# Two ways to transpose q in a Linformer attention and FFN kernel: where each batch's transpose runs, and when it is sent off

## The chip, the cores and the metric

The kernel runs on one core of a Trainium2 chip. The metric is the device time of one execution in microseconds (us), as the median of several runs. A profile of one execution stands beside it; its span is the time from the first to the last instruction.

Names used below: PE or TensorE does matmuls and transposes and writes to PSUM; PEld is its weight load; DVE is VectorE; ACT is ScalarE; POOL is GpSimd, which here issues all loads; SP is SyncE, which here issues the stores and the DMA transposes.

## The reference

Eight batches, eight heads, sequence 1024, head size 64. Keys and values are projected along the sequence from 1024 to 64 rows, then comes plain softmax attention, and its output (8192 tokens x 512) goes through a two-layer FFN with the quick GELU.

```python
k_proj = np.einsum('ks,bhsd->bhkd', E, k)            # 64 x 64 per head
v_proj = np.einsum('ks,bhsd->bhkd', F, v)
scores = np.matmul(q, k_proj.transpose(0, 1, 3, 2)) / np.sqrt(64)
attn   = softmax(scores)                             # over 64 columns
x      = np.matmul(attn, v_proj)                     # heads side by side: 8192 x 512
h      = x @ w_in                                    # 512 x 2048
out    = (h * sigmoid(1.702 * h)) @ w_out            # 2048 x 512
```

## The kernel before

The work is cut into 16 token blocks ("layers" below) of 512 tokens, two to a batch. Layer j runs the first FFN product (`ffn1`, 16 slots of four matmuls of 512 columns, L286) and then the second (`ffn2`, 8 slots of eight matmuls, L297). The attention of later layers is done in the gaps: a list `fill` hangs small pieces behind the slots, `at(j, slot, piece)`. Slots 0 to 15 are those of `ffn1`, O = 16 and up those of `ffn2`. Layer 0 has its `ffn1` cut in two halves, so that its `ffn2` begins at slot Q = 32.

The scores need q with the head dimension on the partitions. For that q has to be transposed. Batch 0 does it on TensorE (`q_tr`), batches 1 to 7 by DMA (`q_dma`):

```python
    def load_q(b):
        qt[b] = ldpool.tile([P, J, H, D], BF16, name="q_sb")
        qv = q[b].rearrange("h (p j) d -> p j h d", p=P)
        for j in range(J):
            nc.gpsimd.dma_start(out=qt[b][:, j], in_=qv[:, j])

    def load(b):
        load_kv(k, kt, b, "k_sb")
        load_q(b)
        load_kv(v, vt, b, "v_sb")
# ...
    def q_tr(g):
        def go():
            if g == 0:
                qT[0] = att.tile([P, J, HP, P], BF16, name="qT")
            t_ps = f_tile([P, 2, HP, P], BF16)
            for jj in range(2):
                for h in range(H):
                    r = h % 2 * D
                    nc.tensor.transpose(t_ps[r:r + D, jj, h // 2, :], qt[0][:, h, 2 * g + jj, :], ident)
            cp = nc.scalar.copy if g == 1 else nc.vector.tensor_copy
            cp(qT[0][:, 2 * g:2 * g + 2], t_ps)
        return go

    def q_dma(b):
        def go():
            qT[b] = att.tile([P, J, HP, P], BF16, name="qT")
            nc.sync.dma_start_transpose(out=qT[b].rearrange("r j p s -> r (j p) s"),
                                        in_=qt[b].rearrange("s j h d -> s (j h d)"))
        return go

    def four(outs, lhsTs, rhss):

        for i, ro in ((0, (LO, HI)), (1, (HI, LO))):
            for ri, r in zip((LO, HI), ro):
                nc.tensor.matmul(outs[i][r], lhsTs[i][ri], rhss[i][ri], start=True, stop=True)

    def scores(h, u):
        b, c = divmod(h, NB2)

        def go():
            if u == 0:
                expT[h] = att.tile([P, HP, TB], BF16, name="expT", bufs=3)
            s_ps = [f_tile([P, TB]) for _ in range(2)]
            four(s_ps, [kts[b % 2][:, 2 * u + i, :] for i in range(2)],
                 [qT[b][:, c * JB:(c + 1) * JB, 2 * u + i, :] for i in range(2)])
            for i in range(2):
                nc.scalar.activation(expT[h][:, 2 * u + i, :], s_ps[i], AF.Exp, scale=scale)
        return go
```

`load(b)` fills the buffers two batches ahead. The pool of `q_sb` has two buffers, so a load waits for the transpose that reads the buffer's former content; `qT` has two buffers as well. The PSUM pool of `f_tile` has four banks, which `ffn1`, `ffn2`, the scores and the transposes share.

The projection of k and v of a batch, and what follows it:

```python
    def proj(b):
        def go():
            kvps[b] = f_tile([P, H, D])
            for j in range(J):
                for e, r in enumerate((LO, HI)):
                    nc.tensor.matmul(kvps[b][r], eft[:, j, e * KP:(e + 1) * KP],
                                     (kt, vt)[e][b][:, :, j, :],
                                     start=(j == 0), stop=(j == J - 1))
        return go
# ...
    def kv_out(b):
        def go():
            ps = kvps.pop(b)
            k_b = att.tile([KP, H, D], BF16, name="k_b")
            nc.vector.tensor_copy(k_b, ps[LO])
            if b > 1:
                nc.sync.dma_start_transpose(out=kts[b % 2], in_=k_b.rearrange("k h d -> k (h d)"))
            v_part(b, ps, slice(0, 2))
            kbs[b] = k_b
        return go
```

From batch 2 on, `k_b` is transposed by a small DMA transpose on the same SyncE queue (`kts`); batch 1 does it on TensorE (`k_tr`).

The places of these pieces:

```python
    at(0, 0, tok(0, 2))
    at(0, 1, tok(0, 3))
    at(0, 4, x_tr(0, 2))
    at(0, 6, x_tr(0, 3))
    at(0, 18, q_tr(2))
    at(0, 20, q_tr(3))
    at(0, Q, scores(1, 0), scores(1, 1), gelu_table)
    for t in range(JB):
        at(0, Q + 2 + t, tok(1, t))
        at(0, Q + 3 + t, x_tr(1, t))
    at(1, 3, q_dma(1))
    at(1, 8, proj(1))
    at(1, 9, kv_out(1))
    at(1, 10, lambda: k_tr(1, kbs[1], 0), q_dma(2))
    for u in range(2):
        at(1, O + u, scores(2, u))
        at(1, O + 3 + u, scores(3, u))
        at(2, O + u, scores(4, u))
        at(2, O + 3 + u, scores(5, u))
    for t in range(JB):
        at(1, O + 2 + t, tok(2, t))
        at(1, O + 3 + t, x_tr(2, t))
    at(2, 1, norm(3, 0))
    at(2, 11, norm(3, 1))
    for b in range(2, B):
        j = max(2, NB2 * b - 3)
        at(j, 2, proj(b))
        at(j, 3, kv_out(b))
        if b > 2:
            at(j, 4, q_dma(b))
    for j in (1, 2):
        at(j, O + 5, gelu_table)
    at(2, O + 5, norm(4, 0))
    at(3, 4, norm(4, 1))
    for j in range(3, NBLK - 2):
        for u in range(2):
            if j + 3 < NBLK:
                at(j, O + 5 * u, scores(j + 3, u))
            at(j, O + 5 * u, norm(j + 2, u))
        if j + 3 < NBLK:
            at(j, O + 6, gelu_table)

# ...
    for j in range(NBLK):
        if j % NB2 == 0 and j // NB2 + 2 < B:
            load(j // NB2 + 2)
        halves = 2 if j == 0 else 1
        for i in range(halves * FC):
            hf, fc = divmod(i, FC)
            ffn1(j, fc, slice(hf * TB // halves, (hf + 1) * TB // halves))
            filled(j, i)
        for s in range(2 * JB):
            ffn2(j, s // 2, s % 2)
            filled(j, halves * FC + s)
```

Of the kernel before, what the change touches and what calls it, by code (L numbers as in the profile page):

```python
# [10 lines left out]
BF16 = mybir.dt.bfloat16  # L11
# [6 lines left out]
def kernel(ctx, tc, q, k, v, E, F,  # L18
                                                     moe_w_in, moe_w_out, out):
    nc = tc.nc  # L20
    B, H, S, D = q.shape
    KP, _ = E.shape
    DM, DFF = moe_w_in.shape
    P = 128
    J = S // P
    NB2 = S // 512
    HP = H // 2
# [10 lines left out]
    att = ctx.enter_context(tc.tile_pool(name="att", bufs=2))  # L38
# [11 lines left out]
    kt, vt, qt = {}, {}, {}  # L50
# [29 lines left out]
    ident = consts.tile([P, P], BF16)  # L80
# [32 lines left out]
    def f_tile(shape, dt=F32):  # L113
        return ps_f.tile(shape, dt, name="f_ps")

    def warm(n):
        w_ps = f_tile([P, TB])
        for _ in range(n):
            nc.tensor.matmul(w_ps, zeros[:, :P], zeros, start=True, stop=True)  # L119
# [6 lines left out]
    t_ps = f_tile([P, J, 2 * KP], BF16)  # L126
# [6 lines left out]
    kvps, kbs, qT, expT, xT = {}, {}, {}, {}, {}  # L133
# [10 lines that stand above are left out]
# [32 lines left out]
# [8 lines that stand above are left out]
            kbs[b] = k_b  # L184
        return go

    def q_tr(g):
        def go():
            if g == 0:
                qT[0] = att.tile([P, J, HP, P], BF16, name="qT")  # L190
            t_ps = f_tile([P, 2, HP, P], BF16)
            for jj in range(2):
                for h in range(H):
                    r = h % 2 * D
                    nc.tensor.transpose(t_ps[r:r + D, jj, h // 2, :], qt[0][:, h, 2 * g + jj, :], ident)
            cp = nc.scalar.copy if g == 1 else nc.vector.tensor_copy
            cp(qT[0][:, 2 * g:2 * g + 2], t_ps)
        return go

    def q_dma(b):  # L200
# [24 lines that stand above are left out]
# [42 lines left out]
    def x_tr(h, t):  # L267
        def go():
            x_sb = xs.pop((h, t)).rearrange("s h d -> s (h d)")
            n_ps = ps_n.tile([P, KC, P], BF16, name="n_ps")  # L270
            for c in range(KC):
                nc.tensor.transpose(n_ps[:, c, :], x_sb[:, c * P:(c + 1) * P], ident)  # L272
            cp = nc.scalar.copy if (h, t) == (0, 0) else nc.vector.tensor_copy
            cp(x_of(h)[:, :, t * P:(t + 1) * P], n_ps)
        return go
# [33 lines left out]
    def at(j, slot, *fs):  # L309
        fill.setdefault((j, slot), []).extend(fs)  # L310

    O = FC
    Q = 2 * FC
# [1 line left out]
        k_half(proj0(0, g), g)  # L315
        warm(3)
    for g in (0, 1):
        q_tr(g)()
    warm(4)
    for u in range(2):  # L320
        scores(0, u)()
# [9 lines left out]
    at(0, 1, tok(0, 3))  # L331
    at(0, 4, x_tr(0, 2))
    at(0, 6, x_tr(0, 3))
    at(0, 18, q_tr(2))
    at(0, 20, q_tr(3))
    at(0, Q, scores(1, 0), scores(1, 1), gelu_table)
    for t in range(JB):
        at(0, Q + 2 + t, tok(1, t))
        at(0, Q + 3 + t, x_tr(1, t))
    at(1, 3, q_dma(1))  # L340
    at(1, 8, proj(1))
    at(1, 9, kv_out(1))
    at(1, 10, lambda: k_tr(1, kbs[1], 0), q_dma(2))
# [10 lines left out]
    for b in range(2, B):  # L354
        j = max(2, NB2 * b - 3)
        at(j, 2, proj(b))
        at(j, 3, kv_out(b))
        if b > 2:
            at(j, 4, q_dma(b))
    for j in (1, 2):  # L360
        at(j, O + 5, gelu_table)
    at(2, O + 5, norm(4, 0))
# [55 lines left out]
```

The softmax here doesn't subtract the row's maximum and nothing guards it: scores larger than these inputs give would overflow.

## Time and profile before

| | |
|---|---|
| time, median of 3 runs | 528.34 us (527.36 to 529.83) |
| profiled span | 527.6 us, 6576 instructions |
| granted TensorE clock, mean | 0.996 |
| eight batches of FFN on TensorE: L297, L286 | 231.8 and 227.2 us busy |
| score, denominator and value matmuls (L211) | 13.6, 10.3 and 10.1 us busy |
| transposes of q: 7 by DMA, time to landing | median 12.4 us |

The page cuts the span into 40 slices of 13.2 us. Each digit is the busy share in tenths:

```profile
PE   6799989999999999999989999999999999999997
PEclk9999998999999999999999999999999999999999
DMA  9999999999999029950299205010150201010102
```

TensorE is near full except at the two ends. The granted clock dips in one slice, the seventh. The DMA engines are full for the first 13 slices (170 us), in which weights and the first batches are loaded, and then busy in bursts.

An idle time that a row shows in brackets is the time in which its engine did nothing just before, with what ended that idle time. Matmuls are pipelined, so the start-to-start distance of rows tells more than the length of one.

### The profile page before, as it was taken

The numbers are of one execution on the slowest core, as the hardware profiler recorded it, in microseconds if no ns is written. First come the engines' busy times: TensorE is split into PE (matmuls) and PEld (weight loads), VectorE is DVE, ScalarE is ACT, GpSimd is POOL, SyncE is SP. The second block draws the span as 40 slices with busy tenths as digits, with TensorE's granted clock in tenths as the row PEclk, the third lists the DMA queues.
The fourth block names the chain that finished last, engine by engine and source line by source line (L and its number), as shares of the span: only waits on it lengthen the run. The fifth ranks groups of instructions, "written<-read, shape, count | busy, mean of one in ns | idle before, by whom it ended". The sixth has DMA issues, their size and how long they took to land.

```text
span 527.6 us, 6576 instructions
## 1 busy us (share of the span) xinstructions
PE 508.6 (96%) x2798; PEld 230.8 (44%) x2798; DVE 243.9 (46%) x206; ACT 264.7 (50%) x433; POOL 75.9 (14%) x94
## 2 busy tenths in 40 slices
PE   6799989999999999999989999999999999999997
PEld 3475434444444444344434444444444444444443
DVE  2411212683966381746718275572818466470000
ACT  1466454465546546364563745556464646334351
POOL 6344314331050000500014000000000000000000
PEclk9999998999999999999999999999999999999999
DMA  9999999999999029950299205010150201010102
GB/s 168 200 203 182 244 141 195 179 208 163 167 132 185 0 81 158 109 136 1 91 155 152 88 2 148 18 80 1 78 88 0 81 0 81 1 80 2 80 0 81
DMA packets 116878, 54.83 MB, mean 104 GB/s; under 512 B 89712, under 2 KB 114288, under 8 KB 114928
## 3 DMA queue, kind: packets, MB, share of 16 engines
q0 software_dynamic: 83328, 29.37, 49.8%
q1 hardware_dynamic: 33440, 24.78, 17.7%
q8 instruction: 22, 0.36, 0.3%
q10 hardware_dynamic: 80, 0.26, 0.2%
q14 instruction: 8, 0.07, 0.0%
HBM read 59.24 MB, written 16.78 MB: 144 GB/s over the span
## 4 chain that ended last, share of the span: by engine, by line
PE 81%; DMA 16%; DVE 1%; POOL 1%; issue 1%; ACT 0%; SPq 0%; ACTq 0%; POOLq 0%
PE f_ps L297 41%; PE f_ps L286 32%; DMA qT<-q_sb 11%; DMA w_in_sb<-in_moe_w_in_dram 5%; PE f_ps L140 2%; PE f_ps L211 2%; PE d_ps L211 1%; PE n_ps L211 1%; DVE vq L173 0%; DVE k_b L180 0%; PE n_ps L272 0%; PE d_ps L257 0%; POOL v_sb L57 0%; POOL k_sb L57 0%; ACT o_sb L300 0%
## 5 line engine op out<-in xcount | busy, mean ns | idle before, releaser
L243 DVE RECIPROCAL rden<-d_ps 128x512 f32<-128x512 f32 x52 | 174.4, 3353 | 153.8 <-PE d_ps L211 153.8
L297 PE MATMUL f_ps<-w_out_sb,gT 128*128 128x512 bf16 x1024 | 231.8, 381 | 0.1
L286 PE MATMUL f_ps<-xT,w_in_sb 128*128 128x512 bf16 (+1 forms) x1088 | 227.2, 367 | 1.2 <-DMA w_in_sb<-in_moe_w_in_dram 0.6
L288 ACT ACTIVATE gT<-f_ps 128x512 bf16<-128x512 f32 (+1 forms) x272 | 155.7, 572 | 87.3 <-PE f_ps L286 86.1
L286 PEld LDWEIGHTS <-w_in_sb 128*128 128x128 bf16 x1088 | 104.8, 98 | 118.5 <-issue 4.9
L297 PEld LDWEIGHTS <-gT 128*128 128x128 bf16 x1024 | 97.8, 98 | 123.4 <-issue 12.9
L300 ACT COPY o_sb<-f_ps 128x512 f32<-128x512 f32 x64 | 37.6, 587 | 140.3 <-PE f_ps L297 130.5
L63 POOL DMA_DIRECT2D q_sb<-in_q_dram x56 | 49.1, 894 | 88.3 <-DMA qT<-q_sb 47.6
L223 ACT ACTIVATE expT<-f_ps 128x512 bf16<-128x512 f32 x64 | 34.7, 600 | 10.9 <-PE f_ps L211 10.8
L244 DVE TENSOR_TENSOR xT<-n_ps,rden 128x512 bf16<-128x512 f32 x52 | 36.0, 692 | 5.5
L57 POOL DMA_DIRECT2D k_sb<-in_k_dram x9 | 7.8, 866 | 102.1 <-PE f_ps L140 98.7
L211 PE MATMUL f_ps<-qT,kt 64*64 64x512 bf16 x128 | 13.6, 404 | 7.5 <-DMA qT<-q_sb 6.9
L223 ACT ACT_TABLE_LOAD x13 | 16.7, 1283 | 5.9 <-PE f_ps L211 5.7
L227 ACT ACT_TABLE_LOAD x14 | 18.0, 1283 | 0.3
L262 DVE RECIPROCAL rd<-d_ps 128x4 f32<-128x4 f32 x24 | 4.2, 175 | 27.2 <-PE d_ps L257 27.2
L140 PE MATMUL f_ps<-k_sb,eft 128*64 128x512 bf16 x56 | 13.4, 382 | 0.0
L140 PE MATMUL f_ps<-v_sb,eft 128*64 128x512 bf16 x56 | 13.4, 382 | 0.0
L211 PEld LDWEIGHTS <-kt 64*64 64x64 bf16 x128 | 3.9, 103 | 21.1 <-issue 17.7
L263 DVE TENSOR_TENSOR x_sb<-d_ps,rd 128x256 bf16<-128x256 f32 x24 | 10.2, 425 | 0.8
L119 PE MATMUL f_ps<-zeros 128*128 128x512 bf16 x30 | 9.4, 450 | 1.2 <-DVE zeros L101 1.2
L211 PE MATMUL d_ps<-expT,ones 64*64 64x512 bf16 x104 | 10.3, 381 | 0.0
L211 PE MATMUL n_ps<-expT,vq 64*64 64x512 bf16 x104 | 10.1, 376 | 0.0
(45 smaller groups left out, 92.3 us busy)
## 6 DMA issues: line engine op xcount, KB each, us to landing
out_dram<-o_sb SPq DMA_DIRECT2D x15, 1024.0 KB, 3.9
k_sb<-in_k_dram POOLq DMA_DIRECT2D x7, 1024.0 KB, 16.8
q_sb<-in_q_dram POOLq DMA_DIRECT2D x56, 128.0 KB, 12.7
v_sb<-in_v_dram POOLq DMA_DIRECT2D x7, 1024.0 KB, 10.8
w_in_sb<-in_moe_w_in_dram POOLq DMA_DIRECT2D x8, 256.0 KB, 14.4
w_out_sb<-in_moe_w_out_dram POOLq DMA_DIRECT2D x4, 512.0 KB, 14.4
k_sb<-in_k_dram POOLq DMA_DIRECT2D x2, 512.0 KB, 7.5
q_sb<-in_q_dram POOLq DMA_DIRECT2D x2, 512.0 KB, 13.7
```

What stands on the lines that cost most here:

```text
L63: nc.gpsimd.dma_start(out=qt[b][:, j], in_=qv[:, j])
L140: nc.tensor.matmul(kvps[b][r], eft[:, j, e * KP:(e + 1) * KP], (kt, vt)[e][b][:, :, j, :], start=(j == 0), stop=(j == J - 1))
L211: nc.tensor.matmul(outs[i][r], lhsTs[i][ri], rhss[i][ri], start=True, stop=True)
L223: nc.scalar.activation(expT[h][:, 2 * u + i, :], s_ps[i], AF.Exp, scale=scale)
L227: nc.scalar.preload_act_table(AF.Gelu_apprx_sigmoid)
L243: nc.vector.reciprocal(rden, d_ps[i])
L244: nc.vector.tensor_tensor(x_of(h)[:, 2 * u + i, :], n_ps[i], rden, op=ALU.mult)
L263: nc.vector.tensor_tensor(xs[h, t][:, 4 * g:4 * g + 4, :], d_ps[:, :, :D], rd.to_broadcast([P, 4, D]), op=ALU.mult)
L286: nc.tensor.matmul(h_ps, w_in_sb[:, kc, fc * P:(fc + 1) * P], xT[j][:, kc, ts], start=(kc == 0), stop=(kc == KC - 1))
L288: nc.scalar.activation(gts[j][:, fc, ts], h_ps, AF.Gelu_apprx_sigmoid)
L297: nc.tensor.matmul(o_ps[0], gts[j][:, fc, n * P:(n + 1) * P], w_out_sb[:, fc, :], start=(fc == 0), stop=(fc == FC - 1))
L300: nc.scalar.copy(osb[j][:, n, :], o_ps[0])
```

## The change

Three things are done. Batch 1's q is transposed on TensorE, in four groups of eight transposes behind slots 2, 4, 6 and 8 of layer 1, with a copy to SBUF by VectorE for each; its DMA transpose goes. The DMA transposes of batches 3 to 7 are sent off at slot O of layer 2b - 4, the second half of the layer in front of the one that projects that batch's k (batch 2's stays at layer 1, slot 10). And the two halves of the scores of token block 1 stand behind two slots in place of one. The aim is that q's transpose is there when the scores want it.

```diff
--- before.py
+++ after.py
@@ -184,17 +184,24 @@
             kbs[b] = k_b
         return go
 
-    def q_tr(g):
+    def q_tr(b, g):
         def go():
             if g == 0:
-                qT[0] = att.tile([P, J, HP, P], BF16, name="qT")
+                qT[b] = att.tile([P, J, HP, P], BF16, name="qT")
             t_ps = f_tile([P, 2, HP, P], BF16)
             for jj in range(2):
-                for h in range(H):
-                    r = h % 2 * D
-                    nc.tensor.transpose(t_ps[r:r + D, jj, h // 2, :], qt[0][:, h, 2 * g + jj, :], ident)
-            cp = nc.scalar.copy if g == 1 else nc.vector.tensor_copy
-            cp(qT[0][:, 2 * g:2 * g + 2], t_ps)
+                j = 2 * g + jj
+                if b == 0:
+                    for h in range(H):
+                        r = h % 2 * D
+                        nc.tensor.transpose(t_ps[r:r + D, jj, h // 2, :], qt[0][:, h, j, :], ident)
+                else:
+                    for p in range(HP):
+                        nc.tensor.transpose(
+                            t_ps[:, jj, p, :],
+                            qt[b][:, j, 2 * p:2 * p + 2, :].rearrange("s t d -> s (t d)"), ident)
+            cp = nc.scalar.copy if b == 0 and g == 1 else nc.vector.tensor_copy
+            cp(qT[b][:, 2 * g:2 * g + 2], t_ps)
         return go
 
     def q_dma(b):
@@ -315,7 +322,7 @@
         k_half(proj0(0, g), g)
         warm(3)
     for g in (0, 1):
-        q_tr(g)()
+        q_tr(0, g)()
     warm(4)
     for u in range(2):
         scores(0, u)()
@@ -331,13 +338,15 @@
     at(0, 1, tok(0, 3))
     at(0, 4, x_tr(0, 2))
     at(0, 6, x_tr(0, 3))
-    at(0, 18, q_tr(2))
-    at(0, 20, q_tr(3))
-    at(0, Q, scores(1, 0), scores(1, 1), gelu_table)
+    at(0, 18, q_tr(0, 2))
+    at(0, 20, q_tr(0, 3))
+    at(0, Q, scores(1, 0))
+    at(0, Q + 1, scores(1, 1), gelu_table)
     for t in range(JB):
         at(0, Q + 2 + t, tok(1, t))
         at(0, Q + 3 + t, x_tr(1, t))
-    at(1, 3, q_dma(1))
+    for g in range(4):
+        at(1, 2 + 2 * g, q_tr(1, g))
     at(1, 8, proj(1))
     at(1, 9, kv_out(1))
     at(1, 10, lambda: k_tr(1, kbs[1], 0), q_dma(2))
@@ -356,7 +365,7 @@
         at(j, 2, proj(b))
         at(j, 3, kv_out(b))
         if b > 2:
-            at(j, 4, q_dma(b))
+            at(NB2 * b - 4, O, q_dma(b))
     for j in (1, 2):
         at(j, O + 5, gelu_table)
     at(2, O + 5, norm(4, 0))
```

## The prediction

> **What bounds the kernel now.** I read the busy shares and the chain of waits on the page first, then the list of who waited for whom, then the timeline of TensorE around each wait that this list names.
>
> ```profile
> PE 508.6 (96%) x2798; PEld 230.8 (44%) x2798; DVE 243.9 (46%) x206; ACT 264.7 (50%) x433; POOL 75.9 (14%) x94
> PE 81%; DMA 16%; DVE 1%; POOL 1%; issue 1%; ACT 0%; SPq 0%; ACTq 0%; POOLq 0%
> PE f_ps L297 41%; PE f_ps L286 32%; DMA qT<-q_sb 11%; DMA w_in_sb<-in_moe_w_in_dram 5%; PE f_ps L140 2%; PE f_ps L211 2%; PE d_ps L211 1%; PE n_ps L211 1%; DVE vq L173 0%; DVE k_b L180 0%; PE n_ps L272 0%; PE d_ps L257 0%; POOL v_sb L57 0%; POOL k_sb L57 0%; ACT o_sb L300 0%
> ```
>
> TensorE is the bound: busy 96%, every other engine at half or less. The chain puts 11% (56 us, as its answer in order of time has 10.6%) on the DMA transposes of q. The reader must not take that as what can be won: the chain follows the transposes back to their issue, and TensorE worked during most of that time. What it lost is in the list of waits (waiter, what was waited for: us in total, times, longest us):
>
> ```profile
> PE f_ps L211 <- DMA qT<-q_sb: 6.9, 4, 2.8
> POOL q_sb L63 <- DMA qT<-q_sb: 47.6, 4, 14.1
> PE f_ps L211 <- ACT expT L223: 0.5, 1, 0.5
> ```
>
> So the score matmuls (L211) stood still for q's transpose four times, 6.9 us in all. The 47.6 us of GpSimd are loads held back because their buffer was still being transposed; they cost nothing unless a matmul waits for what they load. The timeline of TensorE around the first and the fourth wait (start, us, engine, what, in brackets the idle time before):
>
> ```profile
> 75.07 1.89 PE L297 MATMUL f_ps<-w_out_sb,gT 128*128 128x512 bf16 x8
> 79.80 0.64 PE L211 MATMUL f_ps<-qT,kt 64*64 64x512 bf16 x4 [2.84 <-DMA qT<-q_sb]
> 80.37 3.31 PE L297 MATMUL f_ps<-w_out_sb,gT 128*128 128x512 bf16 x8
> 83.61 0.41 PE L211 MATMUL f_ps<-qT,kt 64*64 64x512 bf16 x4
> ```
>
> ```profile
> 271.05 1.89 PE L297 MATMUL f_ps<-w_out_sb,gT 128*128 128x512 bf16 x8
> 274.69 0.41 PE L211 MATMUL f_ps<-qT,kt 64*64 64x512 bf16 x4 [1.75 <-DMA qT<-q_sb]
> 274.91 0.41 PE L211 MATMUL d_ps<-expT,ones 64*64 64x512 bf16 x4
> 275.12 0.41 PE L211 MATMUL n_ps<-expT,vq 64*64 64x512 bf16 x4
> 275.47 4.71 PE L297 MATMUL f_ps<-w_out_sb,gT 128*128 128x512 bf16 x21
> ```
>
> The first wait has a second price: the eight L297 matmuls behind it take 3.31 us in place of 1.89. The granted clock was 0.90 between 80 and 97 us and 1.00 in the stages after it.
>
> **What the Trainium skill says.** "TensorE: Matmul & The Clock Gate", section "Why this matters for your kernels", warns of idle gaps above about 3 us, after which the clock falls to half. The trace agrees roughly: the gap of 2.84 us was followed by matmuls 0.43 us apart, those of 1.11, 1.15 and 1.75 us were followed by the usual 0.22. The same page, "Part 4: PE-mode transpose", gives 275 to 390 ns for a 128x128 bf16 transpose, its latency. Here 128x128 transposes have a mean of 220 ns and overlap, so I cost them by the spacing in the trace. "DMA: Bandwidth & Descriptors", section "Issuing engines are not separate DMA queues", says that transfers issued from SyncE and GpSimd run on the same 16 DMA engines and interleave. The trace agrees: q's transposes landed after 19.3 and 20.7 us beside the loads of the first 100 us, and after 6.7 us at the fastest.
>
> **The change part by part.**
>
> *1. Batch 1's q goes over TensorE.* The DMA transpose of batch 1 was issued at 60.45 us and landed at 79.8; the scores stood ready at about 77. It goes, and with it the first wait. Start to start, 75.07 to 80.37 is 5.30 us; the same eight matmuls and four scores take 114.13 to 116.29 = 2.16 us in the next layer, so 3.14 are lost. The slow eight: 80.37 to 83.61 = 3.24, against 1.82 from 114.13 to 115.95; 1.42 lost. Together **4.56 us won**.
> Added on TensorE: 4 groups of 8 transposes 128x128. Their price from the trace: in the first layer's second half, eight L297 matmuls with four transposes (L272) and four 130-column matmuls (L257) between them repeat every 50.93 to 53.12 = 2.19 us; eight L297 alone are 8 x 0.216 = 1.73; so eight small matmuls cost 0.46 us. Four groups: **1.84 us lost**. They lie on the bound, so all of it counts.
> Added on VectorE: four copies of 128x1024 at 0.69 us (L197), 2.8 us. VectorE stood idle for 10.95 us before the k copy at 68.82, and the gaps between groups are two blocks of L286 (1.73 us), so they hide.
>
> *2. The transposes of batches 3 to 7 start earlier.* Before, batches 3, 4, 5 were issued at 137.7, 200.2 and 262.2 us, slot 4 of a layer, behind kt's small transpose, and landed about 12 us later, while slot 16 comes 11 to 12 us after slot 4. Now each starts at slot 16 of the layer in front, about 30 us before its scores. In the undisturbed layer at 177.78 one stretch from L297 over scores and norm to L297 takes 2.59 us. The three disturbed ones: 147.21 to 150.99 = 3.78 (1.19 lost), 209.11 to 212.93 = 3.82 (1.23), 271.05 to 275.47 = 4.42 (1.83). **4.25 us won.** Batches 6 and 7 had no wait, as no loads run then; nothing is won there.
>
> *3. The two halves of the scores of token block 1 are a slot apart.* Before, the second half waited 0.47 us at 44.71 for the exponential to free a PSUM buffer. From 41.80 to 48.51 (24 L297 and eight scores) are 6.71 us; apart they need 3 x 1.82 + 2 x 0.34 = 6.14. **0.57 us won**.
>
> *Sum:* 4.56 + 4.25 + 0.57 - 1.84 = 7.54 us. The profiled span of 527.6 becomes 520.1; the median of the times lies 0.7 above that span, so 520.8 us, 1.4% less.
>
> **The rivals.**
> *(a) The wait moves to q's load.* Transposes on TensorE stand in its order in front of L286 and would stop the layer. Against it: the last piece of batch 1's q was issued at 48.10 us and landed 6.8 us later, at 54.9; the first group comes after three blocks of the layer, at 58.97 + 3 x 0.865 = 61.6. Slack 6.7 us. If it happened, one or two us would come back: 522 to 523.
> *(b) Batch 2's transpose or kt comes late.* TensorE reaches the scores of batch 2 about 3.3 us earlier. Its transpose was issued at 82.3 us, after its q had landed, took 20.7 us, and was in at 103.0; the scores then began at 115.95. Slack 13 us before, 9.6 after, and without batch 1's transpose on the DMA engines it should be in earlier. The small transpose of kt is tighter: issued at 108.17, in 6.3 us later at 114.5, only 1.5 us ahead of the scores. It hangs on VectorE, which hangs on TensorE, so it shifts along; but if more loads run beside it, a wait of up to 1 us comes: 521.5.
> *(c) The early transposes collide.* Batch 3's now runs at about 109 us, beside loads that kept the DMA engines full until 120. It may take 20 us, as batch 1's and 2's did, and is still in 10 us ahead of its scores. For it speaks that the k, q and v loads of a batch now come in one piece, as q's no longer wait for a transpose (GpSimd's 47.6 us), so that kt's transpose of batches 4 and 5 runs beside more traffic; their slack was about 6 us (issued 198.73, in 6.8 us later, scores due at 211). Cost 0 to 1 us.
> *(d) TensorE is the loser.* If transposes cost their full 220 ns each, 32 are 7.0 us, and nearly the whole gain is gone: 526. Against it the 0.46 us for eight in the trace.
> *(e) The slow clock comes back elsewhere.* It needs a gap of nearly 3 us, and none is left after the start.
>
> **Range and chances.** The centre is 520.8. A better result than 519 would need gains that no wait in the list offers: 6.9 us for q, 0.5 for the exponential, 1.4 of slow clock, and the cost of the transposes cannot be below zero. That bounds it at about 518.8 + noise. The times of before spread from 527.4 to 529.8, so one us of noise either way. On the other side a and b, alone or together, give 522 to 523.5. Range **519.3 to 523.5**. Faster by over 2% means below 517.8, which the list of waits does not hold: 0.04. Within 2%: 0.94. Slower by over 2% needs a new wait of 18 us: 0.02.
>
> **What would show it.** In the profile after: no wait of L211 on qT in the list; eight L297 at about 1.9 us after the first scores of batch 1, and a clock of 1.00 there (part 1). Four rows of x8 transposes on L286's side of layer 1, each moving the next L286 by about 0.46 us; near 1 us each or an idle time on q_sb in front of them would prove rival a or d. At batches 3, 4 and 5 the stretch around the scores is 2.6 us as at 177.78 (part 2); an idle time there on kt proves b or c. The scores of token block 1 without the 0.47 us on ACT (part 3). I am wrong if the span falls by less than 4 us, or if TensorE shows a new wait of over 1 us.

## The result and the profile after

The changed kernel takes 522.43 us (median; 521.51 to 525.26), the kernel before beside it 528.62. The ratio is 0.9892, with an interval of 0.9846 to 0.9939: 1.1% faster. The profiled span fell from 527.6 to 520.0 us. Line numbers have moved by seven: L286 is now L293, L297 is L304, L211 is L218, and the DMA transpose of q is L210.

The busy shares and the chain of waits of the changed kernel:

```profile
PE 509.9 (98%) x2830; PEld 233.1 (45%) x2830; DVE 246.6 (47%) x210; ACT 264.4 (51%) x433; POOL 75.7 (15%) x94
PE 96%; ACT 1%; DMA 1%; DVE 1%; issue 0%; ACTq 0%
```

TensorE was busy for 508.6 us and is now busy for 509.9. So the work on the bound has grown a little, and the idle time beside it fell from 19.0 to 10.1 us. The chain no longer passes through any DMA transpose; it runs along TensorE almost from end to end.

The longest waits of TensorE, and the one of GpSimd that belongs to q (waiter, what was waited for: us in total, times, longest us):

```profile
PE f_ps L119 <- DVE zeros L101: 1.2, 1, 1.2
PE f_ps L128 <- ACT ef_sb L123: 1.1, 1, 1.1
PE f_ps L162 <- DVE k_b L155: 1.0, 2, 0.5
...
POOL q_sb L63 <- DMA qT<-q_sb: 19.9, 1, 19.9
```

The 6.9 us of L211 on qT and the 0.5 us on the exponential are gone. What is left of TensorE's waits belongs to the start of the kernel.

The timeline of TensorE in layer 1, where batch 1's transposes stand (L200), and at the place of the first wait:

```profile
60.86 0.61 PE L200 MATMUL f_ps<-ident,q_sb 128*128 128x128 bf16 x8
61.31 1.89 PE L293 MATMUL f_ps<-xT,w_in_sb 128*128 128x512 bf16 x8
...
76.15 1.89 PE L304 MATMUL f_ps<-w_out_sb,gT 128*128 128x512 bf16 x8
77.97 0.41 PE L218 MATMUL f_ps<-qT,kt 64*64 64x512 bf16 x4
78.32 1.90 PE L304 MATMUL f_ps<-w_out_sb,gT 128*128 128x512 bf16 x8
80.15 0.41 PE L218 MATMUL f_ps<-qT,kt 64*64 64x512 bf16 x4
```

A row says 0.61 us for eight transposes, but the next L293 starts 0.45 us after the first transpose: that distance is the price. From 76.15 to 78.32 are 2.17 us (before: 5.30), and the eight L304 from 78.32 to 80.15 take 1.83 (before: 3.24).

The stretch of batch 5, which had the longest of the three later waits:

```profile
265.19 1.89 PE L304 MATMUL f_ps<-w_out_sb,gT 128*128 128x512 bf16 x8
267.01 0.41 PE L218 MATMUL f_ps<-qT,kt 64*64 64x512 bf16 x4
267.25 0.39 PE L218 MATMUL d_ps<-expT,ones 64*64 64x512 bf16 x4
267.46 0.39 PE L218 MATMUL n_ps<-expT,vq 64*64 64x512 bf16 x4
267.78 8.81 PE L304 MATMUL f_ps<-w_out_sb,gT 128*128 128x512 bf16 x40
```

From 265.19 to 267.78 are 2.59 us; before, the same stretch took 4.42.

### The profile page after: what moved, and what is told of

It is laid out like the page before. It is cut to its first block, busy times and chain, and to the rows that moved or that the text cites. A ratio compares the mean times of both kernels' runs of the same rounds, so it can differ in the third digit from the quotient of the medians.

```text
span 520.0 us, 6643 instructions
## 1 busy us (share of the span) xinstructions
PE 509.9 (98%) x2830; PEld 233.1 (45%) x2830; DVE 246.6 (47%) x210; ACT 264.4 (51%) x433; POOL 75.7 (15%) x94
## 4 chain that ended last, share of the span: by engine, by line
PE 96%; ACT 1%; DMA 1%; DVE 1%; issue 0%; ACTq 0%
PE f_ps L304 43%; PE f_ps L293 43%; PE f_ps L140 2%; PE f_ps L218 2%; PE d_ps L218 1%; PE n_ps L218 1%; DMA ef_f<-in_E_dram 1%; PE d_ps L264 1%; PE n_ps L279 1%; ACT expT L230 1%; PE f_ps L119 0%; PE f_ps L197 0%; PE f_ps L149 0%; PE f_ps L200 0%; DVE x_sb L270 0%; ACT L234 0%
## 5 line engine op out<-in xcount | busy, mean ns | idle before, releaser
L304 PE MATMUL f_ps<-w_out_sb,gT 128*128 128x512 bf16 x1024 | 230.6, 379 | 0.1
L293 PE MATMUL f_ps<-xT,w_in_sb 128*128 128x512 bf16 (+1 forms) x1088 | 228.4, 368 | 0.7 <-DVE xT L281 0.6
L293 PEld LDWEIGHTS <-w_in_sb 128*128 128x128 bf16 x1088 | 105.4, 98 | 116.9 <-issue 4.9
L304 PEld LDWEIGHTS <-gT 128*128 128x128 bf16 x1024 | 97.2, 98 | 122.4 <-issue 11.3
L218 PE MATMUL f_ps<-qT,kt 64*64 64x512 bf16 x128 | 13.2, 399 | 0.1
L204 DVE COPY qT<-f_ps 128x1024 bf16<-128x1024 bf16 x7 | 4.8, 691 | 16.3 <-PE f_ps L200 8.8
L119 PE MATMUL f_ps<-zeros 128*128 128x512 bf16 x30 | 10.1, 480 | 1.2 <-DVE zeros L101 1.2
L218 PE MATMUL d_ps<-expT,ones 64*64 64x512 bf16 x104 | 10.2, 382 | 0.0
L218 PE MATMUL n_ps<-expT,vq 64*64 64x512 bf16 x104 | 10.0, 376 | 0.0
## 6 DMA issues: line engine op xcount, KB each, us to landing
k_sb<-in_k_dram POOLq DMA_DIRECT2D x7, 1024.0 KB, 15.9
```

The source lines that it names most:

```text
L293: nc.tensor.matmul(h_ps, w_in_sb[:, kc, fc * P:(fc + 1) * P], xT[j][:, kc, ts], start=(kc == 0), stop=(kc == KC - 1))
L304: nc.tensor.matmul(o_ps[0], gts[j][:, fc, n * P:(n + 1) * P], w_out_sb[:, fc, :], start=(fc == 0), stop=(fc == FC - 1))
```

## The experiments

The theory: the gain is a sum of separate waits on TensorE, each removed by its own part of the change, less the transposes added there. The rivals: the DMA engines are one shared bottleneck, so that the parts act on one another; or it is the order in SyncE's queue, and not how early a transpose is asked for, that made them late.

### Batch 1 alone

```diff
-    at(0, Q, scores(1, 0))
-    at(0, Q + 1, scores(1, 1), gelu_table)
+    at(0, Q, scores(1, 0), scores(1, 1), gelu_table)
...
-            at(NB2 * b - 4, O, q_dma(b))
+            at(j, 4, q_dma(b))
```

> The changed kernel with only its first part: batch 1's q on TensorE; the DMA transposes of batches 3 to 7 back at slot 4 and the scores of token block 1 together. Theory (the gain is a sum of separate waits): span 527.6 - 4.5 + 1.9 = 525.0 us; the first wait and the slow clock behind it are gone, the three waits on qT at batches 3, 4 and 5 stay at 1.1 to 1.8 us each. Rival (the DMA engines are one shared bottleneck, so taking batch 1's transpose off them also brings the later ones in earlier): the three waits shrink below 0.5 us and the span is 522 or less.

Measured: span 524.0 us; ratio to before 0.994 (0.992 to 0.996). The waits on qT in its profile:

```profile
PE f_ps L218 <- DMA qT<-q_sb: 2.9, 3, 1.2
```

Batch 1's wait is gone, the other three are there. They add up to 2.9 us where they were 4.0 (1.11, 1.15 and 1.75), and that is the 1 us by which the span is below the expected 525.0. So the waits are nearly separate. The shared DMA engines account for about 1 us at most, and perhaps for less: in another profile, with batch 1 still by DMA, the same three add up to 3.4 us (the gap filled, below: 3.9 in all, less 0.5). The rival's 522 was not reached.

### The earlier DMA transposes alone

```diff
-            at(j, 4, q_dma(b))
+            at(NB2 * b - 4, O, q_dma(b))
```

> The kernel before with only the DMA transposes of batches 3 to 7 sent off a layer earlier; batch 1 still by DMA. Theory: span 527.6 - 4.2 = 523.4 us; the wait of 2.8 us at batch 1 with the slow eight matmuls behind it stays, the other three are gone. Rival (one shared bottleneck): the earlier transposes press on the DMA engines, the first wait grows and the gain is under 3 us.

Measured: span 521.8 us; ratio 0.9891 (0.9835 to 0.9946). The three later waits are gone, the first one stays. The timeline of TensorE around it:

```profile
75.06 1.89 PE L297 MATMUL f_ps<-w_out_sb,gT 128*128 128x512 bf16 x8
79.91 0.41 PE L211 MATMUL f_ps<-qT,kt 64*64 64x512 bf16 x4 [2.96 <-DMA qT<-q_sb]
80.25 1.90 PE L297 MATMUL f_ps<-w_out_sb,gT 128*128 128x512 bf16 x8
82.08 0.41 PE L211 MATMUL f_ps<-qT,kt 64*64 64x512 bf16 x4
```

The gap is as long as before, even a little longer (2.96 against 2.84 us), but the eight matmuls behind it run at full speed: 80.25 to 82.08 are 1.83 us, not 3.24. That is 1.4 of the 1.6 us by which the span is below 523.4. The slow clock behind the gap is therefore not a fixed price of the gap.

Do the two parts add up? The ratios don't show it: 0.6% and 1.1% alone, 1.1 to 1.2% for the whole change, and the second of them may be anything from 0.5 to 1.7%. The best spans on one chip fit a sum: 524.9 us before, 523.4 with batch 1 alone, 521.4 with the earlier DMA transposes alone, 519.9 for the changed kernel. That is 1.5 and 3.5 us alone and 5.0 together; the third part, 0.6 us, lies within the scatter and had no run of its own.

### The gap filled

```diff
+    at(1, O, lambda: warm(10))
     for u in range(2):
         at(1, O + u, scores(2, u))
```

> The kernel before with ten matmuls on zeros (L119's kind) in front of the first scores of batch 1, 10 x 0.216 = 2.2 us in a gap of 2.8 us. They compute nothing that is used. Theory (the idle gap itself costs the clock behind it, in some runs): the clock stays at 1.00 behind the wait in every run, the wait on qT shrinks to about 0.7 us, its end does not move (79.8), so the span falls by up to 1.4 us against a run in which the clock fell, and by 0 against one in which it did not. Rival (the slow eight matmuls had another cause, such as the load of the DMA engines): eight matmuls at 3.3 us behind the wait again.

Measured: span 525.3 us; ratio to before 0.9991 (0.9974 to 1.0009). The ten matmuls on zeros in the timeline of TensorE:

```profile
77.00 2.32 PE L119 MATMUL f_ps<-zeros 128*128 128x512 bf16 x10
79.82 0.41 PE L211 MATMUL f_ps<-qT,kt 64*64 64x512 bf16 x4 [0.50 <-DMA qT<-q_sb]
80.16 1.90 PE L297 MATMUL f_ps<-w_out_sb,gT 128*128 128x512 bf16 x8
```

The scores start at 79.82, as before at 79.80: matmuls in this wait cost nothing. No slow matmuls follow. But over many runs the time is the same as before. If each run had lost 1.4 us to the clock at this place, the ratio would be 0.9973, just outside that interval; the ratio itself stands for 0.5 us. The mean granted clock of the runs compared says the same, 0.9958 with the gap filled and 0.9960 before. So the slow clock behind the gap does not come in full in every run; how often it comes is not shown. Whether the gap causes it where it occurs is left open: two other profiles with this gap (2.96 us above, 2.64 us in the next experiment) don't have it either.

### One place further ahead in the queue

```diff
-        at(j, 3, kv_out(b))
         if b > 2:
-            at(j, 4, q_dma(b))
+            at(j, 2, q_dma(b))
+        at(j, 3, kv_out(b))
```

> The kernel before, with one line moved two slots: the DMA transposes of q of batches 3 to 7 stand at slot 2 in place of slot 4 of the same layer, so in SyncE's queue in front of kt's small transpose and no longer behind it. Theory (the queue's order makes them late: behind kt they wait for VectorE to write k_b, 5 us into the layer, though their data is long there): they start at the layer's begin, right behind the output store, kt follows once they are issued, and both are in before the scores; the three waits on qT are gone, the first one at batch 1 stays, span 527.6 - 4.2 = 523.4. Rival (the whole layer ahead is needed, as kt behind a transpose of 7 to 10 us is late in its place): waits of 1 us or more at batches 3 to 5, now on kt, span 526 to 529.

Measured: span 523.4 us; ratio 0.993 (0.9906 to 0.9954). SyncE's queue at batch 4, first in the kernel before, then here (start, us of the issue, what):

```profile
194.16 0.33 SPq L305 DMA_DIRECT2D out_dram<-o_sb  x1
198.73 1.18 SPq L182 DMA_TRANSPOSE kt<-k_b  x1
200.21 9.76 SPq L203 DMA_TRANSPOSE qT<-q_sb  x1
```

```profile
193.03 0.33 SPq L305 DMA_DIRECT2D out_dram<-o_sb  x1
193.71 6.89 SPq L203 DMA_TRANSPOSE qT<-q_sb  x1
200.71 1.28 SPq L182 DMA_TRANSPOSE kt<-k_b  x1
```

Before, q's transpose stood behind kt's, which waits for VectorE to write `k_b`. In front of it, it goes 0.7 us behind the output store and not 6.1. It was in after 12.7 us, at 206.4; kt after 7.9 us, at 208.6; the scores started at 209.80 with no wait. All three later waits are gone with a move of two slots, so it was the queue's order that made them late; a layer's distance is not needed. The slack is only 1.2 us for kt; the layer's distance of the change gives more. The first wait (2.64 us) stays, as expected. That the span is 523.4 to the digit is luck: this profile lacks the 1.4 us of slow clock behind the gap, and layer 0 ends 1.9 us later than before (its output store goes at 61.67 and not at 59.79).

### Batch 1 by DMA, ahead of the store

```diff
-    for g in range(4):
-        at(1, 2 + 2 * g, q_tr(1, g))
+    at(0, Q + 5, q_dma(1))
```

> The changed kernel, but batch 1's q goes by DMA after all, with its transpose put into SyncE's queue in layer 0, in front of that layer's output store. Theory (before, batch 1's transpose was late because it stood behind the output store in SyncE's queue: the store went at 59.8 us, q was in at 54.9): the transpose starts at about 55, is in at 74 to 75 after some 19 us, the scores are due at about 76, so there is no wait and the 1.9 us of transposes on TensorE are saved: span 518.1, ratio to before about 0.982. Rival (the DMA engines are too full there, the transpose takes longer or the queue was not what held it): a wait on qT of 1 to 4 us with slow matmuls behind it, span 520 to 524.

Measured: span 518.1 us, median time 520.02; ratio 0.9834 (0.9788 to 0.9881). SyncE's queue and TensorE at the scores:

```profile
54.86 13.90 SPq L210 DMA_TRANSPOSE qT<-q_sb  x1
68.82 0.59 SPq L312 DMA_DIRECT2D out_dram<-o_sb  x1
```

```profile
74.43 1.89 PE L304 MATMUL f_ps<-w_out_sb,gT 128*128 128x512 bf16 x8
76.25 0.41 PE L218 MATMUL f_ps<-qT,kt 64*64 64x512 bf16 x4
76.59 1.90 PE L304 MATMUL f_ps<-w_out_sb,gT 128*128 128x512 bf16 x8
```

The transpose starts at 54.86, when the last of its q has landed, and is in 20.3 us later, at 75.2. The scores at 76.25 don't wait. The output store goes 9 us later than before (68.82 against 59.79), which nothing waits for. The 1.9 us of transposes on TensorE are saved: this version's span is 1.9 below the changed kernel's (best spans on one chip: 517.9 and 519.9). Its slack is 1.1 us, so a slower load could bring the wait back.

### The transposes on TensorE twice

```diff
-                    for p in range(HP):
+                    for p in [*range(HP)] * 2:
```

> The changed kernel with each of batch 1's transposes on TensorE done twice into the same place: 64 in place of 32. Theory (0.46 us for eight, all on the bound): span 1.9 us above the changed kernel's, so 521.9 with a good start of the clock, each group 0.9 us in place of 0.45. Rival (they cost less than they look, as VectorE's copy or the GELU behind them is what the next matmuls wait for): under 0.5 us more; rival (their full 220 ns count): 7 us more.

Measured: span 522.2 us; ratio to before 0.9931 (0.9905 to 0.9957). A group in its timeline:

```profile
61.34 1.06 PE L200 MATMUL f_ps<-ident,q_sb 128*128 128x128 bf16 x16
62.24 1.89 PE L293 MATMUL f_ps<-xT,w_in_sb 128*128 128x512 bf16 x8
```

From 61.34 to 62.24 are 0.90 us for sixteen, against 0.45 for eight: 56 ns for each. The span lies 2.2 us above 520.0, where 1.9 were expected; 0.5 of it stands at the start (layer 0's second product begins at 42.22 us and not at 41.74). Both rivals fall: the cost is neither hidden behind VectorE's copy nor 220 ns each.

### The changed kernel once more, and a start that keeps the clock

> The changed kernel once more, beside the others on the same chip. Theory: span 520.0 and no wait on qT; ratio to before 0.986. Its times in the first comparison spread from 521.5 to 525.3; if that spread is only the clock's start, spans with a mean clock of 0.99 lie 2 to 4 us above those at 1.00.

Measured: median time 523.39 us; ratio 0.9881 (0.9828 to 0.9934). The profiled span is 523.8; the spans of the other runs go from 519.9 to 523.3. The three runs with a mean clock of 0.99 have spans of 522.7 to 523.8, the other three (0.996 to 1.000) 519.9 to 520.5: the spread goes with the clock. Busy time and granted clock (the number behind POOL's) in the first three stretches of 10 us, in the changed kernel's first profile and in this one:

```profile
0.00:10.00 10.00, 7.67 (x32) 3.18 (x32) 2.70 (x10) 1.90 (x2) 7.80 (x15) 1.00 0.90 159
10.00:20.00 10.00, 8.34 (x84) 4.95 (x83) 2.57 (x7) 4.43 (x7) 3.08 (x5) 1.00 1.35 203
20.00:30.00 10.00, 8.02 (x67) 5.99 (x67) 5.66 (x19) 3.72 (x11) 4.48 (x6) 0.83 1.45 195
```

```profile
0.00:10.00 10.00, 6.49 (x24) 2.85 (x25) 2.69 (x10) 1.90 (x2) 7.81 (x15) 0.88 0.85 158
10.00:20.00 10.00, 8.38 (x82) 4.91 (x81) 2.10 (x6) 2.86 (x5) 3.00 (x5) 0.95 1.34 202
20.00:30.00 10.00, 7.99 (x53) 5.18 (x51) 5.29 (x19) 3.67 (x8) 4.58 (x6) 0.74 1.45 197
```

The second has a slow clock in all three stretches. Layer 0's second product starts at 44.68 us in it and at 41.74 in the first: 2.9 us lost. The first has a slow stretch too, behind idle times of 0.61 us at most in the 10 us in front of it. Four matmuls take as long there as eight of the same kind a little later:

```profile
23.79 1.01 PE L293 MATMUL f_ps<-xT,w_in_sb 128*128 128x256 bf16 x4 [0.61 <-DVE xT L281]
28.16 1.04 PE L293 MATMUL f_ps<-xT,w_in_sb 128*128 128x256 bf16 x8
```

It cost nothing: before, with a clock of 1.00 in this stretch, the second product started at 41.80. The other 0.8 us of the difference of 3.8 between the two profiles stand at the first scores of batch 2:

```profile
116.30 0.41 PE L218 MATMUL f_ps<-qT,kt 64*64 64x512 bf16 x4 [0.79 <-DMA kt<-k_b]
```

There kt's transpose took 8.6 us to land; in the first profile it took 6.2. This is the rival of the prediction that named kt, in one profile of two.

To see whether the start explains the spread, the version with batch 1 ahead in the queue was given a few more matmuls on zeros:

```diff
-    warm(12)
+    warm(16)
...
     tok(0, 0)()
+    warm(2)
     tok(0, 1)()
     x_tr(0, 0)()
     x_tr(0, 1)()
+    warm(2)
```

> Batch 1's transpose ahead in the DMA queue, as in the kernel that reached a span of 518.1, and besides 16 in place of 12 matmuls on zeros at the start, and two of them in each of two gaps of 0.6 us before layer 0. Theory (the runs of one kernel differ by up to 5 us because the clock is slow in the first 35 us of some of them, after gaps of 2 us there): the spread of the spans falls under 1.5 us and the median span is 517.5 to 518.5. Rival (the spread comes from elsewhere): spans of 518 to 521 as before, or 1 us more for the added matmuls.

Measured: spans of 518.0 to 518.3 us, where the same version without them had 517.9 to 520.8; median time 520.04, ratio 0.9843 (0.9815 to 0.9871). The best run is not better, and among these five runs no slow start is left: all have a mean clock of 0.999 or 1.000. They ran on another chip than the six they are set against; on their own chip the kernel with the transposes twice, which has the old start, had a clock of 0.993 in four runs of five. So the start accounts for the spread, as far as five runs can show it; which of the added matmuls did it is not shown. Layer 0's second product starts at 41.79, as in the good runs: a small delay at the start is absorbed, since layer 0 then waits for its weights anyway (0.3 us here, 0.9 in the version without the added matmuls).

## Why the prediction was right, point by point

- *Bound and waits: right.* TensorE is the bound, its list of waits holds what could be won, and the chain's 11% on the DMA transposes was no measure of it.
- *First wait, 3.14 us: right.* 5.30 - 2.17 = 3.13 in the profile after.
- *Slow clock behind it, 1.42 us: right in that profile, not confirmed as a part of the mean.* The profile gave 3.24 - 1.83 = 1.41. But gaps of 2.96 and 2.64 us had no such price, and filling the gap left the mean time where it was (ratio 0.9991). The term should have been counted with a chance below one. Without it the sum is 6.1 us. The medians differ by 6.2; the interval of the ratio, some 3 to 8 us, can't tell the two sums apart, and the best spans seen are 524.8 and 519.7, 5.1 apart. The Trainium skill, "TensorE: Matmul & The Clock Gate", section "What's actually happening", says that the window in which activity is judged is free-running, so that the number of slow matmuls at a kernel's start differs from run to run. Three gaps of 2.64 to 2.96 us, of which one was followed by slow matmuls, fit that, but no run tests it.
- *Transposes on TensorE, 1.84 us: right.* The four groups cost 0.45, 0.44, 0.45 and 0.54 = 1.88 us, and doubling them gave 0.90 for a group. The rival of 220 ns each fell.
- *Three later waits, 4.25 us: the size right, the mechanism half right.* The stretches now take 2.60, 2.60 and 2.59 us (4.23 won). But I wrote that each transpose starts at slot 16 of the layer in front, some 30 us ahead. SyncE's queue knows no slots: batch 4's was issued at 160.83, right behind the output store at the start of that layer, 45 us ahead of its scores at 206.29. A slot only fixes the place in the queue. That the place was the cause I had half seen ("behind kt's small transpose"); the move by two slots shows it.
- *Scores a slot apart, 0.57 us: right.* The same matmuls take 41.74 to 47.81 = 6.07 us, 0.64 less than before.
- *Rival a (q's load): did not come.* The transposes begin with no wait.
- *Rival b (kt late): came in one of two profiles of the changed kernel,* 0.79 us, within the 1 us I gave it.
- *Rival c: no cost, but its reason was wrong in part.* Batch 3's transpose, issued at 106.19, took 20.6 us and was in 19 us ahead of its scores. I said that q's loads no longer wait for a transpose. One still does, 19.9 us: the load of batch 3's q began at 90.89, right after batch 2's DMA transpose was in (issued at 74.43, 15.9 us). So it seems to have been given batch 2's buffer and not that of batch 1. No matmul waited for that load.
- *Rival e: did not come, but its reason was wrong.* I said that a slow clock needs a gap of nearly 3 us. Behind the start no slow stretch came while matmuls ran, but in the start one came after idle times of 0.61 us at most, and gaps of 2.96 and 2.64 us passed without one: such a gap is neither needed nor enough.
- *The time:* 522.43 against 520.8, inside the range. The profiled span was met (520.0 against 520.1), and its terms add up: 3.13 + 1.41 + 4.23 + 0.64 - 1.88 = 7.53 of 7.6 us. That both profiles had starts that cost nothing (second product at 41.80 and 41.74) was luck. What was mis-sized is the step from the span to the median, 0.7 us. A run's time lies 1.7 to 1.8 us above its own span; the 0.7 came about because the profile before is of a run of 529.35 us, 1.0 above the median. The profile after is of a run of 521.73, 0.7 below the median: two of the four runs have a slower clock (0.990 and 0.993) and spans of 523.5 and 521.3.

## What to carry to other kernels

A late DMA in a queue is first a question of what stands in front of it: look at the order of issues on that queue, and at what the entry in front waits for, before work is moved to the engine that is the bound. Here a reordering did for batch 1 what 1.9 us of TensorE had bought. Count a slow clock seen in a single profile as a chance, not as a price, and read what can be won from the bound engine's own waits, start to start.

## What was not expected of the hardware

- The clock behind a gap of nearly 3 us fell in one profile (2.84 us) and not in two others (2.96 and 2.64 us).
- A gap of 2.3 us near the start was followed by matmuls at half speed (four of 512 columns took 1.91 us, and 1.03 in the profile where that gap was 1.1). Runs of one kernel differ by 3 us with such starts; with eight matmuls on zeros more, the spans of five runs lay within 0.3 us, where six runs without them had 2.9.
- The DMA transpose of a batch's q, the same bytes each time, took 4.9 and 4.7 us to issue with no load or store beside it (batches 6 and 7 of the kernel before), 6.9 right behind an output store (batches 4 to 7 of the changed kernel), and up to 15.0 beside loads.
